# Reordering accumulating loads, sums of x and sums of weights in a pooled-attention and expert-mixture kernel

## The chip, the cores and the metric

The kernel runs on one core of a Trainium2 chip. The metric is the device time of one execution in microseconds (us), and lower is better. Quoted times are medians unless something else is said. PE is TensorE, PEld its weight loads, DVE is VectorE, ACT is ScalarE, POOL is GpSimd, SP is SyncE.

## The reference, cut to what matters

```python
def _attn_ref(q, k, v):                    # 8 batches x 8 heads, 576 rows, 64 columns
    k_p = k.reshape(B, H, Sp, 8, D).mean(axis=3)      # 72 pooled keys
    v_p = v.reshape(B, H, Sp, 8, D).mean(axis=3)      # 72 pooled values
    attn = softmax(q @ k_p.T / sqrt(D))
    return attn @ v_p

def _moe_ref(x, domain_probs, w1, w2):     # x 4608 x 512, 4 experts, 1024 hidden
    p = domain_probs / domain_probs.sum(-1)
    for e in range(4):
        out += p[:, e:e + 1] * (np.maximum(x @ w1[e], 0) @ w2[e])
```

The output of the attention is x of the mixture of experts.

## The kernel before

The two products of an expert are each done in seven smaller products instead of eight, which needs sums and differences of the operands beforehand. They are made by DVE: `weight_sums` and `first_weight_sums` of the weights, `x_sum` of x, `hidden_sums` of the hidden layer. All go through `combine`, a two-input DVE operation whose operands lie in SBUF.

The long middle of the kernel is a loop over slots. A slot holds one of the seven products of the "up" layer, in two halves, and one of the "down" layer of the expert before. 28 slots are one chunk of x (four experts), and under them runs the attention of the next batch: its loads, key and value sums, scores and contexts are hung onto slots by number. The engines each work in the order in which the program issues, so the slot number of a piece decides what stands ahead of it.

```python
def combine(dst, a, op, b):
    nc.vector.tensor_tensor(out=dst, in0=a, in1=b, op=op)

def load_part(b, what, part):      # parts 1.. add onto part 0, so each waits for the last
    src, raw = ((k, raw_k), (v, raw_v))[what]
    nc.gpsimd.dma_start(out=raw[:], in_=rows_of(src, b, 2 * part, 2 * part + 2),
                        accum_op=ALU.add if part else ALU.bypass)

def fold_keys(b, hs):              # (cut) two-input DVE operations in SBUF
    for dup in range(2):
        nc.vector.tensor_add(out=kp_all[0:SP, hs, dup, :], in0=raw[:, hs, 0, :],
                             in1=raw[:, hs, 1, :])

def hidden_sums(c, e, part):
    a11, a12, a21, a22 = quarters(c, e)
    if part == 0:
        combine(S3[:], a11, ALU.subtract, a21)      # called S below, 128x1024
    ...                                             # cut: parts 1 to 3

def down(c, e, step, flip=0, pooled=()):
    ...                                             # cut: eight matmuls into ps
    if step == 0:
        nc.scalar.copy(out=chains[(1 + flip) % 2][:], in_=chains[flip][:])
    elif step in pooled and e > 0:                  # pooled is (4,)
        for j in range(BLOCKS):
            prob = p_all[:, c * NR + row * BLOCKS + j, e:e + 1]
            nc.scalar.activation(out=addend[:, j], in_=ps[:, j], func=ACT.Copy, scale=prob)
        dst = acc[:, row * BLOCKS:(row + 1) * BLOCKS, cols]
        nc.gpsimd.tensor_add(out=dst, in0=dst, in1=addend[:])   # "the add of the step"
    else:
        ...                                         # cut: the same by DVE, from PSUM

# the slot loop, cut
for g in range(7 * N + 1):
    t, i = divmod(g, 7)
    if i in (0, 2, 3) and t < N:
        hidden_sums(*below_of[t], i)
    ...                                             # cut: two halves of an up product
    down(*below_of[t2], i2, t2 % 2, POOLED)
    for piece in later.get(g, ()):                  # attention of the next batch
        piece()
    for piece in sums.get(g, ()):                   # sums of weights
        piece()
```

Of each 28 slots, slots 5, 19 and 26 hold a `down` whose sum GpSimd adds. The add in slot 5 belongs to the last expert of the chunk before. GpSimd also issues the loads: a load that waits for an earlier landing holds up everything behind it in GpSimd's order.

The softmax here doesn't subtract the row's maximum and nothing guards it: scores larger than these inputs give would overflow.

## Time and profile before

| | before |
|---|---|
| time, median of 3 runs (range) | 500.82 us (499.92 to 501.33) |
| profiled span, granted clock | 498.8 us, 0.999 |
| PE busy, weight loads busy | 98%, 82% |
| DVE, ACT, POOL busy | 77%, 61%, 23% |

First the page of the profile. The busy line gives each engine's microseconds, its share and its instruction count. The chain of waits tells which engine's work ended last at each step. The last line is the group of GpSimd's adds of the step: 24 of them, 32.6 us in all, 1360 ns each.

```profile
PE 489.9 (98%) x4663; PEld 406.8 (82%) x4663; DVE 382.3 (77%) x756; ACT 303.3 (61%) x561; POOL 115.2 (23%) x112
...
PE 88%; DVE 9%; ACT 1%; issue 1%; ACTq 0%; DVEq 0%
...
L738 POOL TENSOR_TENSOR acc<-acc,addend 128x512 f32<-128x512 f32 x24 | 32.6, 1360 | 257.3 <-ACT addend L736 182.8
```

PE is the engine that bounds the kernel, but DVE holds 9% of the chain, which means places where PE waited for something that DVE delayed. The Trainium skill, page "Perfetto Trace Analysis", section "Identifying the Most-Contended Engine", advises MFU and the weight loads' busy share rather than matmul busy time. Here what is sought is below 1% of the time and lies in a few places. A share of the whole span doesn't say where they are: weight loads are busy 81.6% of the span. MFU was not worked out. The measure used here is the pace. In the steady stage a group of eight 128x256 matmuls starts 0.87 us after the group before, and any longer distance is a pause. Read so, PE paused 0.80 us at 245-247, 1.38 us at 298-300, 0.85 us at 437-441, 0.30 at 113, 0.32 at 85 and 0.49 at 67 and 75 together.

Each line is one stretch: its length, then busy time and instructions of PE, PEld, DVE, ACT and POOL, then clock and DMA.

```profile
core 0: us, PE busy (x) PEld busy (x) DVE busy (x) ACT busy (x) POOL busy (x), PEclk, DMA share, GB/s
...
95.00:130.00 35.00, 34.87 (x343) 29.93 (x343) 32.11 (x68) 22.34 (x40) 12.93 (x11) 1.00 0.73 71
...
230.00:285.00 55.00, 54.52 (x521) 47.23 (x520) 44.36 (x86) 35.05 (x66) 16.02 (x14) 1.00 0.65 81
285.00:340.00 55.00, 53.95 (x540) 46.34 (x538) 43.40 (x84) 35.46 (x66) 13.90 (x11) 1.00 0.55 73
340.00:440.00 100.00, 99.46 (x958) 87.60 (x956) 75.08 (x147) 61.49 (x118) 7.71 (x6) 1.00 0.13 30
```

Between 285 and 340 us PE lacks 1.05 us of a full stretch, between 230 and 285 it lacks 0.48. (Busy time hides a part, because the records overlap: that of a group lasts 1.03 us, and the next group starts 0.87 us after it. The pace is counted from start to start and does not.)

The timeline tells why. Columns are start, length, engine, line, operation, output and inputs, count, and in brackets the idle time before it with what ended that.

```profile
238.84 1.43 POOL L151 DMA_DIRECT2D kraw<-in_k_dram  x1 [1.31 <-DMA kraw<-in_k_dram]
...
239.69 0.84 ACT L736 ACTIVATE addend<-o_ps,p_all 128x256 f32<-128x256 f32 x2 [0.77 <-PE o_ps L724]
...
241.85 1.42 POOL L151 DMA_DIRECT2D vraw<-in_v_dram  x1 [1.58 <-DMA vraw<-in_v_dram]
...
242.60 2.52 DVE L242 TENSOR_TENSOR S<-H 128x1024 bf16<-128x1024 bf16 x1
242.71 1.84 POOL L738 TENSOR_TENSOR acc<-acc,addend 128x512 f32<-128x512 f32 x1
...
245.04 0.68 DVE L637 CUSTOM_DVE_ANT_0 H<-unit,partial 128x512 bf16<-128x512 f32 x1
...
245.80 0.57 ACT L669 COPY unit<-unit 128x512 f32<-128x512 f32 x1 [0.73 <-DVE H L637]
...
246.43 0.60 PE L656 MATMUL unit<-xT,w_bf 128*128 128x256 bf16 x4 [0.30 <-ACT unit L669]
...
247.21 1.03 PE L724 MATMUL o_ps<-w_bf,H 128*128 128x256 bf16 x8 [0.19 <-ACT o_ps L732]
```

ACT had the addend ready at 240.53 (239.69 + 0.84). GpSimd could not add it, for its queue held the third part of the values ahead of it, and that waited until 241.85 for the part before to land. So the add ran at 242.71. In that moment DVE began S, which then took 2.52 us. Everything behind S on DVE came late: the relu sum (L637), then ACT's copy of a PSUM bank (L669), and PE waited 0.30 us for that copy and 0.19 us for another. The same stood at 295, and S was worse there, although its record begins 0.69 us before that of the add:

```profile
294.91 1.40 POOL L151 DMA_DIRECT2D vraw<-in_v_dram  x1 [0.77 <-DVE acc L799]
...
295.08 3.08 DVE L242 TENSOR_TENSOR S<-H 128x1024 bf16<-128x1024 bf16 x1
...
295.77 1.83 POOL L738 TENSOR_TENSOR acc<-acc,addend 128x512 f32<-128x512 f32 x1
```

At 435 us it was a sum of x (128x512) that met the add; the same operation took 0.42 us when alone:

```profile
435.55 1.37 POOL L738 TENSOR_TENSOR acc<-acc,addend 128x512 f32<-128x512 f32 x1 [11.51 <-DVE H L637]
435.71 1.49 DVE L242 TENSOR_TENSOR xs<-x_rem,xs 128x512 bf16<-128x512 bf16 x1
```

At 109 us batch 3's key sums ran ahead of the add and were not held (0.75 us for two):

```profile
109.40 0.75 DVE L285 TENSOR_TENSOR kp<-kraw 72x512 bf16<-72x512 bf16 x2
...
110.07 0.68 DVE L242 TENSOR_TENSOR w_bf<-w_bf 128x1024 bf16<-128x1024 bf16 x1
110.16 1.72 POOL L738 TENSOR_TENSOR acc<-acc,addend 128x512 f32<-128x512 f32 x1 [5.01 <-DVE kp L285]
```

### The profile page before, as it was taken

To read this page: it belongs to the slowest core of one execution; us is meant where nothing else is said; L and a number is where in the kernel's file an instruction comes from. 1 tells how busy PE (TensorE), PEld (TensorE's weight loads), DVE (VectorE), ACT (ScalarE), POOL (GpSimd) and SP (SyncE) were. 2 spreads that over 40 slices of the span, in tenths; PEclk is the share of its full clock that TensorE was granted. 3 is DMA by queue.
4 is the path that set the end of the run, shared out by engine and by line. 5 is a ranking of instruction groups with operands and counts; after the bars stand their busy time and mean duration, and the time that the engine had idled before them with its cause. 6 is when DMAs were issued, how large, how long until landed. Compare 5 with 4: busy or idle time off the path is not lost.

```text
span 498.8 us, 11453 instructions
## 1 busy us (share of the span) xinstructions
PE 489.9 (98%) x4663; PEld 406.8 (82%) x4663; DVE 382.3 (77%) x756; ACT 303.3 (61%) x561; POOL 115.2 (23%) x112
## 2 busy tenths in 40 slices
PE   8999999999999999999999999999999999999996
PEld 5856458888888888888789878888888888888885
DVE  5567799899768976798769887896678766886674
ACT  4666536865775568556765666566665566556650
POOL 8320413233432164015501262111000100001010
PEclk9999999999999999999999999999999999999999
DMA  9999996987794569154945396220311010004003
GB/s 201 208 204 204 203 164 86 122 69 96 89 129 39 89 68 156 28 78 47 168 48 77 37 117 100 43 57 22 75 23 23 21 64 1 13 22 85 1 1 84
DMA packets 101779, 41.95 MB, mean 84 GB/s; under 512 B 73808, under 2 KB 100176, under 8 KB 101728
## 3 DMA queue, kind: packets, MB, share of 16 engines
q0 software_dynamic: 56896, 22.42, 39.8%
q1 hardware_dynamic: 43728, 17.77, 16.9%
q10 hardware_dynamic: 1104, 1.05, 0.6%
q8 instruction: 36, 0.59, 0.5%
q14 instruction: 15, 0.12, 0.1%
HBM read 45.69 MB, written 9.44 MB: 111 GB/s over the span
## 4 chain that ended last, share of the span: by engine, by line
PE 88%; DVE 9%; ACT 1%; issue 1%; ACTq 0%; DVEq 0%
PE o_ps L724 37%; PE unit L656 36%; PE unit L583 5%; DVE acc L799 3%; PE att L382 1%; PE o_ps L750 1%; DVE S L242 1%; PE unit L332 1%; PE att L435 1%; PE unit L782 1%; DVE H L637 1%; DVE wt_bf L242 1%; DVE x_tok L398 1%; DVE xs L242 1%; PE unit L598 0%
## 5 line engine op out<-in xcount | busy, mean ns | idle before, releaser
L799 DVE SCALAR_TENSOR_TENSOR acc<-o_ps,p_all,acc 128x256 f32<-128x256 f32 (+1 forms) x285 | 127.0, 486 | 55.3 <-PE o_ps L724 36.1
L724 PEld LDWEIGHTS <-H 128*128 128x128 bf16 x1320 | 129.0, 98 | 17.1 <-issue 1.2
L656 PEld LDWEIGHTS <-w_bf 128*128 128x128 bf16 x1024 | 97.7, 98 | 17.6 <-issue 6.1
L637 DVE CUSTOM_DVE_ANT_0 H<-unit,partial 128x512 bf16<-128x512 f32 x128 | 87.7, 685 | 24.7 <-PE unit L656 20.2
L724 PE MATMUL o_ps<-w_bf,H 128*128 128x256 bf16 x792 | 102.6, 272 | 0.5 <-ACT o_ps L732 0.4
L656 PE MATMUL unit<-xT,w_bf 128*128 128x256 bf16 x672 | 96.4, 273 | 1.3 <-ACT unit L669 1.3
L738 POOL TENSOR_TENSOR acc<-acc,addend 128x512 f32<-128x512 f32 x24 | 32.6, 1360 | 257.3 <-ACT addend L736 182.8
L671 ACT COPY partial<-unit 128x512 f32<-128x512 f32 x128 | 72.0, 590 | 32.8 <-PE unit L656 32.6
L656 PEld LDWEIGHTS <-wu_bf 128*128 128x128 bf16 x768 | 73.3, 98 | 10.0 <-issue 1.5
L656 PE MATMUL unit<-xs,wu_bf 128*128 128x256 bf16 x512 | 76.9, 273 | 0.0
L724 PE MATMUL o_ps<-wt_bf,H 128*128 128x256 bf16 x528 | 68.4, 273 | 0.0
L724 PEld LDWEIGHTS <-S 128*128 128x128 bf16 x528 | 51.7, 98 | 6.4
L677 ACT ACTIVATE H<-unit 128x512 bf16<-128x512 f32 x64 | 38.2, 597 | 29.3 <-PE unit L656 29.0
L673 ACT ACTIVATE H<-unit 128x512 bf16<-128x512 f32 x64 | 38.8, 606 | 27.4 <-PE unit L656 27.4
L669 ACT COPY unit<-unit 128x512 f32<-128x512 f32 x64 | 37.3, 582 | 19.3 <-PE unit L656 14.9
L656 PE MATMUL unit<-xs,w_bf 128*128 128x256 bf16 x256 | 38.5, 273 | 0.0
L797 ACT ACTIVATE acc<-o_ps,p_all 128x256 f32<-128x256 f32 x72 | 30.3, 472 | 12.0 <-PE o_ps L724 10.4
L151 POOL DMA_DIRECT2D kraw<-in_k_dram x20 | 25.4, 1270 | 42.1 <-DMA kraw<-in_k_dram 42.1
L724 PE MATMUL o_ps<-w_bf,S 128*128 128x256 bf16 x264 | 34.2, 273 | 0.0
L724 PE MATMUL o_ps<-wt_bf,S 128*128 128x256 bf16 x264 | 34.2, 273 | 0.0
L656 PE MATMUL unit<-xT,wu_bf 128*128 128x256 bf16 x224 | 33.6, 272 | 0.0
L151 POOL DMA_DIRECT2D vraw<-in_v_dram x20 | 26.9, 1343 | 22.6 <-DMA vraw<-in_v_dram 21.8
(148 smaller groups left out, 522.3 us busy)
## 6 DMA issues: line engine op xcount, KB each, us to landing
out_dram<-acc SPq DMA_DIRECT2D x32, 256.0 KB, 4.2
w_bf<-in_moe_w_dram POOLq DMA_DIRECT2D x7, 1024.0 KB, 24.1
q_sb<-in_q_dram POOLq DMA_DIRECT2D x7, 512.0 KB, 9.7
vraw<-in_v_dram POOLq DMA_DIRECT2D x22, 144.0 KB, 5.8
kraw<-in_k_dram POOLq DMA_DIRECT2D x21, 144.0 KB, 5.3
w_bf<-in_moe_w_dram POOLq DMA_DIRECT2D x2, 512.0 KB, 8.5
wt_bf<-in_k_dram POOLq DMA_DIRECT2D x2, 288.0 KB, 6.7
wt_bf<-in_v_dram POOLq DMA_DIRECT2D x4, 144.0 KB, 5.1
```

The lines of the kernel that those rows point to most:

```text
L151: nc.gpsimd.dma_start(out=raw[:], in_=rows_of(src, b, 2 * part, 2 * part + 2), accum_op=ALU.add if part else ALU.bypass)
L583: nc.tensor.matmul(out_ps, lhsT=w1_bf[:, e, kc, fc * P:(fc + 1) * P], rhs=xT[:, kc, at], start=(kc == 0), stop=(kc == KC - 1), skip_group_ ...
L637: nc.vector._custom_dve(TENSOR_ADD_SAT, out=dst, in0=ps, in1=part, s0=LARGEST, s1=0.0)
L656: nc.tensor.matmul(ps[:, n * HN:(n + 1) * HN], lhsT=lhs[:, kc, f:f + P], rhs=rhs[:, kc, :], start=(not grows and n == 0 and kc == 0), stop ...
L669: nc.scalar.copy(out=units[unit][1][:], in_=ps)
L671: nc.scalar.copy(out=part[:, step - 2], in_=ps)
L673: nc.scalar.activation(out=quarter(0, 0), in_=ps, func=ACT.Relu)
L677: nc.scalar.activation(out=quarter(0, 1), in_=ps, func=ACT.Relu)
L724: nc.tensor.matmul(ps[:, j], lhsT=lhs[:, i, j * P:(j + 1) * P], rhs=rhs[:, i, :], start=(not grows and i == 0 and j == 0), stop=(i == HF - 1),
L738: nc.gpsimd.tensor_add(out=dst, in0=dst, in1=addend[:])
L797: nc.scalar.activation(out=dst, in_=o_ps, func=ACT.Copy, scale=prob)
L799: nc.vector.scalar_tensor_tensor(out=dst, in0=o_ps, scalar=prob, in1=dst, op0=ALU.mult, op1=ALU.add,)
```

## The change

The intent is to let GpSimd's add of the step run before the later load parts of the same slot, so that it is over when DVE's S begins; to bring the sums of x ahead of the add in the last slots; and to spread sums of weights, which stood in bunches around batch 1's contexts, singly over DVE's idle places. No work is added or removed: both kernels have 11453 instructions.

```diff
--- before.py
+++ after.py
@@ -850,6 +850,8 @@
                 if 4 <= i < 7:
                     sums[1][i - 4]()
                     sums[2][i - 4]()
+                if i == 5:
+                    sums[1][3]()
                 if i == 6:
                     fold_keys(1, every)
         down(0, 0, 6)
@@ -878,8 +880,10 @@
         load_q_rem(0)
         load_q_rem(1)
         load_wide(1, 2)
+        each(*weight_sums(1)[0:1])
         down_plain(0, 1, 0)
         scores(1, 3)
+        each(*weight_sums(1)[1:2])
         down_plain(0, 1, 1)
         context(1, 0)
         down_plain(0, 1, 2)
@@ -888,14 +892,13 @@
         down_plain(0, 1, 3)
         context(1, 2)
         turn(1, 1)
-        each(*weight_sums(1)[0:2])
         down_plain(0, 2, 0)
         context(1, 3)
         turn(1, 2)
-        each(*weight_sums(1)[2:3], sums[1][3])
+        each(*weight_sums(1)[2:3])
         down_plain(0, 2, 1)
         turn(1, 3)
-        each(*weight_sums(3)[0:2])
+        each(*weight_sums(3)[0:3])
         down_plain(0, 2, 2)
         each(*(lambda n=n: x_sum(1, n) for n in range(4)))
 
@@ -909,15 +912,15 @@
 
         usual = dict(
             queries=-8, keys=-9, values=-2, scores=(-1, 3, 5, 6), contexts=(11, 14, 18, 21),
-            q=1, k=(-2, 0, 3, 6), v=(-2, 0, 3, 6), x=(22, 25, 25, 26), rem=(-3, 17, 24, 25),
+            q=1, k=(-2, 0, 5, 9), v=(-2, 0, 5, 9), x=(22, 25, 25, 25), rem=(-3, 17, 24, 25),
         )
         plans = {b: usual for b in range(BUSY, B + 1)}
         plans[BUSY] = dict(
-            queries=0, keys=4, values=12, scores=(11, 12, 13, 15), contexts=(16, 18, 20, 21),
-            q=6, k=(5, 8, 11, 14), v=(13, 16, 19, 24), x=(24, 26, 26, 26), rem=(0, 6, 8, 14),
-        )
-        plans[B] = dict(usual, x=(25, 25, 26, 26), rem=(-3, 17, 21, 22))
-        plans[BUSY + 1] = dict(usual, values=4, v=(5, 8, 11, 14))
+            queries=0, keys=4, values=12, scores=(11, 12, 13, 15), contexts=(16, 18, 19, 21),
+            q=6, k=(5, 8, 11, 14), v=(13, 16, 19, 24), x=(24, 25, 25, 25), rem=(0, 6, 8, 14),
+        )
+        plans[B] = dict(usual, x=(24, 24, 25, 25), rem=(-3, 17, 21, 22))
+        plans[BUSY + 1] = dict(usual, values=4, v=(5, 8, 12, 16))
 
         for b, plan in plans.items():
             start = 7 * E * (b - BUSY)
@@ -991,7 +994,7 @@
         later = pieces_later()
         below_of = [(0, 3)] + order
         sums = {}
-        for at, pieces in (((5, 3), weight_sums(3)[2:]), ((7,), first_weight_sums(2)[3:]), ((8,), weight_sums(1)[3:]), ((12, 15, 22, 19), weight_sums(2)),
+        for at, pieces in (((3,), weight_sums(3)[3:]), ((7,), first_weight_sums(2)[3:]), ((8,), weight_sums(1)[3:]), ((12, 15, 22, 19), weight_sums(2)),
                            ((15,), first_weight_sums(3)[3:])):
             for slot, piece in zip(at, pieces, strict=True):
                 sums.setdefault(slot, []).append(piece)
```

## The prediction

> **What bounds it now.** TensorE (PE): 98% of the 498.8 us span, granted clock 0.999; the chain of waits is 88% PE. In the steady stage eight 128x256 matmuls start every 0.87 us, so only PE's pauses can be won, and each passes whole to the end (VectorE, DVE, is 77% busy). From the timeline I took, per group of matmuls, the next start minus this start minus the normal pace. The pauses are: 0.80 us at 245-247, 1.38 at 298-300, 0.85 at 437-441, 0.3 at 113, 0.3 at 85, 0.5 together at 67 and 75. Sum 4.1 us. (The fill until 34 us is left alone.)
>
> **Why they pause.** The two large ones are a collision. GpSimd's add of the step (acc+addend, 1.27 us alone) stood in its queue behind the third parts of keys and values, each of which waits for the landing of the part before. The addend was ready at 240.5, but the add ran 242.71-244.55, just when DVE began the S difference (both inputs in SBUF): 2.52 us instead of 0.68; at 295.1, 3.08. At 190 the same op took 1.75 us with no pause behind it. What stands behind S frees a PSUM bank late (PE waits for ScalarE's unit copy, 0.3 and 0.86 us). At 435.7 the last x sum took 1.49 instead of 0.42 for the same reason. The Trainium skill ("SBUF — State Buffer", section "Who interferes with whom") says that a DVE instruction with two SBUF inputs contends with a GpSimd instruction that reads SBUF and that the loser blocks wholly. The trace agrees: all five long ops overlap an add; 28 DVE differences of this size that overlap only a load's issue took 0.69 us at most.
>
> **What the change does.** No work added or removed.
> - Loads go behind the add: it should run at about 240.6-241.9 and 293.1-294.4, ahead of S at 242.6 and 295.1. Wins 0.80+1.38. Parts 3 and 4 start a few us later, still over 10 us before their fold.
> - x one slot sooner: the sums of the last chunk end before the add at 435.4. Its transpose has landed by about 429.7, the sums want it at 432. Wins 0.85.
> - Weight sums spread: about 1.3 us of DVE work moves into its idle gaps at 42, 56 and 58 us. Wins most of the 0.5 at 67/75 and, with one sum out of the stretch at 83, the 0.3 at 85. Context one slot sooner: wins 0.2-0.3 at 113.
> - Loss expected, 0.5 us: near 110 us the earlier context pushes batch 3's key copies (two SBUF inputs) into the add at 110.0, blocking DVE up to 1 us where it is 98% busy.
>
> Net 3.6 us of 500.8 (0.7%): **497.2 us, 80% range 496.0 to 499.2**; faster by over 2%: 0.01, within 2%: 0.98, slower by over 2%: 0.01.
>
> **What would show it.** The slot's adds near 189, 241, 293 us last about 1.3 us; every S difference 0.7 us; no PE wait on ScalarE's unit copy near 245, 298, 437; the x sums at 433 each 0.42 us; PE's pauses after 60 us below 1 us in all.
>
> **What would make it wrong.** The add collides with another two-input DVE op (the slot's x sums, key copies), moving the pause rather than curing it; a moved weight sum delays a PSUM release (68-75 us) or an x sum waits for its transpose; or pauses I read as additive were absorbed later.

## The result

| | before | after |
|---|---|---|
| time, median (range), 6 runs each | 501.1 (499.92 to 501.33) | 497.53 us (497.28 to 498.73) |
| profiled span, granted clock | 498.8, 0.999 | 495.8 us, 0.998 |
| ratio of fast runs, 95% interval | | 0.9938 (0.9923 to 0.9952) |

The six of the kernel before include the three quoted above, which is why its median differs from theirs. A ratio is the mean time of one kernel's fast runs over that of the other's in the same rounds, so it is not quite the ratio of the medians: the ratio says 3.1 us of 501, the medians differ by 3.57 us. The prediction's 497.2 us is 0.3 us below the median measured, and its range holds it.

The page after: PE's share of the chain rose to 95%, DVE's fell to 2%, and the mean add is 95 ns shorter.

```profile
PE 488.6 (99%) x4663; PEld 407.1 (82%) x4663; DVE 377.1 (76%) x756; ACT 302.7 (61%) x561; POOL 114.4 (23%) x112
...
PE 95%; DVE 2%; ACT 1%; issue 1%; ACTq 0%
...
L738 POOL TENSOR_TENSOR acc<-acc,addend 128x512 f32<-128x512 f32 x24 | 30.4, 1265 | 258.3 <-ACT addend L736 201.3
```

Windows after, in the same columns. The two stretches from 230 to 340 us and the one from 340 to 440 us are now full. The one from 95 to 130 us lost 0.66 us of PE's busy time (34.87 before).

```profile
95.00:130.00 35.00, 34.21 (x336) 29.49 (x334) 32.44 (x66) 21.91 (x39) 12.37 (x11) 1.00 0.75 71
...
230.00:285.00 55.00, 55.00 (x529) 47.99 (x527) 42.69 (x86) 35.72 (x68) 16.05 (x15) 1.00 0.69 83
285.00:340.00 55.00, 55.00 (x552) 47.40 (x552) 42.56 (x86) 35.96 (x67) 13.77 (x11) 1.00 0.53 72
340.00:440.00 100.00, 100.00 (x964) 88.46 (x965) 74.97 (x149) 62.27 (x119) 7.61 (x6) 1.00 0.11 30
```

The slot at 241 us. The add follows its addend at once and takes 1.26 us; both loads come behind it; S takes 0.68 us; PE has no wait at 245-247.

```profile
240.70 1.26 POOL L738 TENSOR_TENSOR acc<-acc,addend 128x512 f32<-128x512 f32 x1 [3.17 <-ACT addend L736]
...
241.91 1.42 POOL L151 DMA_DIRECT2D kraw<-in_k_dram  x1
...
242.64 0.68 DVE L242 TENSOR_TENSOR S<-H 128x1024 bf16<-128x1024 bf16 x1
242.81 1.97 POOL L151 DMA_DIRECT2D vraw<-in_v_dram  x1
...
243.24 0.69 DVE L637 CUSTOM_DVE_ANT_0 H<-unit,partial 128x512 bf16<-128x512 f32 x1
...
245.01 0.59 ACT L669 COPY unit<-unit 128x512 f32<-128x512 f32 x1
...
246.44 1.04 PE L724 MATMUL o_ps<-w_bf,H 128*128 128x256 bf16 x8
```

Note the load issue that began 0.17 us after S and lay over it and the relu sum behind it: neither got longer. At 433 us the last sum of x ends before the add begins:

```profile
432.33 0.42 DVE L242 TENSOR_TENSOR xs<-x_rem,xs 128x512 bf16<-128x512 bf16 x1
...
433.42 1.27 POOL L738 TENSOR_TENSOR acc<-acc,addend 128x512 f32<-128x512 f32 x1 [11.51 <-DVE H L637]
```

At 109-113 us stands something new. The add now begins 0.14 us ahead of batch 3's key sums, these take 1.74 us, and the relu sum behind them releases ACT's copy late; PE waits 0.79 us for it.

```profile
109.42 1.26 POOL L738 TENSOR_TENSOR acc<-acc,addend 128x512 f32<-128x512 f32 x1 [4.13 <-ACT addend L736]
109.56 1.74 DVE L285 TENSOR_TENSOR kp<-kraw 72x512 bf16<-72x512 bf16 x2
...
111.83 0.67 DVE L637 CUSTOM_DVE_ANT_0 H<-unit,partial 128x512 bf16<-128x512 f32 x1
...
112.59 0.57 ACT L669 COPY unit<-unit 128x512 f32<-128x512 f32 x1 [2.41 <-DVE H L637]
113.21 1.03 PE L656 MATMUL unit<-xT,w_bf 128*128 128x256 bf16 x8 [0.79 <-ACT unit L669]
```

To put a number on each place, I compared the start of the same group of matmuls in both profiles, and took how much that shift changes between marks chosen in stretches without pauses. Because the shift stays constant between the places named, each pause passed whole to the end. The fill (until 34 us) is left out: its shift is anything from -0.26 to +0.82 us among the profiles, by chance.

| profile against before's, us | 34-92: weight sums | 92-124: keys at 110 | 124-228: S at 190 | 228-281: S at 243 | 281-335: S at 295 | 418-487: x sum at 435 | sum |
|---|---|---|---|---|---|---|---|
| after | -0.68 | +0.80 | -0.03 | -0.80 | -1.37 | -0.84 | -2.92 |

### The profile page after: what moved, and what is told of

The parts are those of the page before. It is cut to its first block, busy times and chain, and to the rows that moved or that the text cites. A ratio compares the mean times of both kernels' runs of the same rounds, so it can differ in the third digit from the quotient of the medians.

```text
span 495.8 us, 11453 instructions
## 1 busy us (share of the span) xinstructions
PE 488.6 (99%) x4663; PEld 407.1 (82%) x4663; DVE 377.1 (76%) x756; ACT 302.7 (61%) x561; POOL 114.4 (23%) x112
## 3 DMA queue, kind: packets, MB, share of 16 engines
q10 hardware_dynamic: 1104, 1.05, 0.6%
## 4 chain that ended last, share of the span: by engine, by line
PE 95%; DVE 2%; ACT 1%; issue 1%; ACTq 0%
PE o_ps L724 40%; PE unit L656 39%; PE unit L583 5%; PE o_ps L750 3%; PE att L382 2%; PE unit L332 1%; PE unit L782 1%; PE att L435 1%; DVE acc L799 1%; PE unit L598 0%; PE unit L306 0%; DVE H L637 0%; DVE kp L285 0%; PE att L489 0%; PE att L472 0%
## 5 line engine op out<-in xcount | busy, mean ns | idle before, releaser
L738 POOL TENSOR_TENSOR acc<-acc,addend 128x512 f32<-128x512 f32 x24 | 30.4, 1265 | 258.3 <-ACT addend L736 201.3
L151 POOL DMA_DIRECT2D vraw<-in_v_dram x20 | 29.3, 1466 | 24.1 <-DMA vraw<-in_v_dram 23.8
```

## The experiments

The theory: GpSimd's add and a two-input DVE operation hold each other up; for S this costs PE time when the add stands directly behind a load in GpSimd's queue; four parts of the change (loads, sums of x, weight sums, context) act separately. The rivals: that the load traffic or its issue slows DVE, with the add a bystander; that the gain of the loads comes from the other moves; that a busy GpSimd is enough, whatever it does. Each kernel was correct, and each is compared with runs of the kernel before on the same chip. The table above continued, from one profile each (sums can be 0.01 off by rounding):

| profile against before's, us | 34-92 | 92-124 | 124-228 | 228-281 | 281-335 | 418-487 | sum |
|---|---|---|---|---|---|---|---|
| loads alone | 0 | 0 | -0.03 | -0.80 | -1.37 | 0 | -2.21 |
| all but the loads | -0.68 | +0.80 | +0.91 | 0 | -0.43 | -0.85 | -0.25 |
| weight sums alone | -0.68 | 0 | +0.01 | -0.15 | -1.36 | 0 | -2.19 |
| context alone | 0 | +0.80 | +0.34 | -0.28 | 0 | 0 | +0.86 |
| last x sums alone | 0 | disturbed | +0.52 | -0.12 | -1.36 | -0.85 | - |
| before, three adds by DVE | 0 | 0 | +0.25 | -0.80 | -1.37 | -0.85 | -2.77 |
| after, add delayed | -0.68 | +0.80 | -0.03 | -0.81 | -1.36 | -0.85 | -2.93 |
| after, keys and a weight sum later | -0.68 | +0.12 | -0.03 | -0.80 | -1.37 | -0.84 | -3.61 |
| after, keys later | -0.70 | +0.80 | -0.03 | -0.80 | -1.36 | -0.85 | -2.94 |
| after, three pieces moved | -0.84 | -0.28 | -0.03 | -0.81 | -1.36 | -0.85 | -4.17 |

### The loads alone, on the kernel before

```diff
-            q=1, k=(-2, 0, 3, 6), v=(-2, 0, 3, 6), x=(22, 25, 25, 26), rem=(-3, 17, 24, 25),
+            q=1, k=(-2, 0, 5, 9), v=(-2, 0, 5, 9), x=(22, 25, 25, 26), rem=(-3, 17, 24, 25),
-        plans[BUSY + 1] = dict(usual, values=4, v=(5, 8, 11, 14))
+        plans[BUSY + 1] = dict(usual, values=4, v=(5, 8, 12, 16))
```

> The kernel before with only the parts of keys and values moved behind the add (slots 5 and 9 in place of 3 and 6). Theory (collision of GpSimd's add with VectorE's S difference): the pauses of PE near 246 and 299 us vanish, the adds of those steps last 1.27 us and every S difference 0.7 us; the pauses at 67, 75, 85, 113 and 437 stay. Shift against before: 0 until 240, -0.8 after 250, -2.2 after 302 and at the end, about 498.9 us where before is 501.1. Rival (the gain is spread over the whole change, the loads only change when DMA traffic comes): under 1 us, or shifts that begin elsewhere than at 245 and 298.

Measured: 498.3 us (498.02 to 499.03), ratio 0.9963 (0.9947 to 0.9979), which is 1.9 us. S took 0.68 us at 242.69, and the two pauses at 245 and 298 are gone. The loads alone are the larger part of the gain, and no other place changed.

### All but the loads

```diff
-            q=1, k=(-2, 0, 5, 9), v=(-2, 0, 5, 9), x=(22, 25, 25, 25), rem=(-3, 17, 24, 25),
+            q=1, k=(-2, 0, 3, 6), v=(-2, 0, 3, 6), x=(22, 25, 25, 25), rem=(-3, 17, 24, 25),
-        plans[BUSY + 1] = dict(usual, values=4, v=(5, 8, 12, 16))
+        plans[BUSY + 1] = dict(usual, values=4, v=(5, 8, 11, 14))
```

> The changed kernel with the loads put back to slots 3 and 6. Theory: the two collisions come back, S differences of about 2.5 and 3.1 us (and 1.75 near 190 without a pause), so 2.2 us slower than the changed kernel, about 499.7; it keeps -0.7 until 109, loses it at 113, and wins 0.85 at 437. Rival (the moved sums have given VectorE enough slack to swallow a late S): no pause at 246 and 299 although S is long, time as the changed kernel within 0.5 us.

Measured: 500.53 us (499.62 to 500.97), ratio 1.0002 (0.9987 to 1.0018). The other moves alone gain nothing measurable: -0.68 and -0.85 are eaten by the +0.80 at 113 us and the +0.91 at 190 us. For with the old order of the loads, S was held at 190 too (1.97 us beyond its 0.68), at 243 the same as before (1.85) and at 295 less (1.96). Its slot at 244 us:

```profile
244.28 2.53 DVE L242 TENSOR_TENSOR S<-H 128x1024 bf16<-128x1024 bf16 x1
244.40 1.84 POOL L738 TENSOR_TENSOR acc<-acc,addend 128x512 f32<-128x512 f32 x1
```

So with the old load order, how far S is held varies from one execution to the next; what goes with it is shown in the section on why the prediction was right or wrong.

### The add delayed, in the kernel after

```diff
             dst = acc[:, row * BLOCKS:(row + 1) * BLOCKS, cols]
+            if e == E - 1 and c in (3, 4):
+                for _ in range(2):
+                    nc.gpsimd.tensor_copy(out=addend[:], in_=addend[:])
             nc.gpsimd.tensor_add(out=dst, in0=dst, in1=addend[:])
```

> The changed kernel, loads left behind the add, but in the fourth expert's step of chunks 3 and 4 GpSimd first copies the addend onto itself twice (same result), so that the add starts about 2 us later, near S again. Theory (it is the add's moment that counts, not the order of the loads): S differences there of about 2 us or more, PE pauses of 0.5 to 1.4 us each, 1.2 to 2.6 us slower than the changed kernel. Rival (what counts is where the loads stand in the queue and when they run): S stays at 0.7 us, no pause, time as the changed kernel.

Measured: 497.3 us (497.27 to 498.09), ratio 0.9945 (0.9930 to 0.9959); no pause. This is a miss as an experiment. The delay brought the add only 0.55 us ahead of S, so S was held for 0.58 us, and that much is absorbed:

```profile
242.56 1.27 POOL L741 TENSOR_TENSOR acc<-acc,addend 128x512 f32<-128x512 f32 x1
...
243.11 1.26 DVE L242 TENSOR_TENSOR S<-H 128x1024 bf16<-128x1024 bf16 x1
```

It gives points of the rule below, but it tells the theories apart no further. An add with no load ahead of it could hardly have done more: it lasts 1.27 us, and S ends 0.55 us after it, so an S of 0.68 us can lose at most about 1.1 us to it (an estimate from these three numbers). The rule below puts what is absorbed at 1.03 us.

### The add held longer, in the kernel after (run twice)

```diff
             dst = acc[:, row * BLOCKS:(row + 1) * BLOCKS, cols]
+            if e == E - 1 and c in (3, 4):
+                nc.gpsimd.tensor_copy(out=addend[:], in_=addend[:])
+                nc.gpsimd.tensor_add(out=addend[:], in0=addend[:], in1=addend[:])
+                nc.gpsimd.tensor_scalar_mul(out=addend[:], in0=addend[:], scalar1=0.5)
             nc.gpsimd.tensor_add(out=dst, in0=dst, in1=addend[:])
```

> After the miss of the late add (S only 0.58 us long over its normal time, no pause): so far six collisions with S fit one rule, pause of PE = S's excess minus 1.03 us (excess 1.84 gave 0.80, 2.40 gave 1.38, 1.07 at 190 and 0.58 in the last run gave none). Now GpSimd has four ops in a row there, copy, doubling, halving (exact), add, so that it is at work from 241.2 to about 245.0 while S comes at 243.1; loads stand behind as in the changed kernel. Theory: S waits to the end of the last, excess about 1.9 us, pause about 0.85 us at each of the two places, 1.7 us slower than the changed kernel, with the loads in the changed order. Rival (order and time of the loads): S at most 0.6 us long over normal and no pause. Open: whether S can slip in between two GpSimd ops; then the excess is about 0.6 us or less and nothing is told apart.

Measured: five runs at 497.53 to 498.47 us and one, the profiled one, at 1023.01 us: TensorE went at about half pace in it (0.50 us a matmul of 256 columns in place of 0.27), with a granted clock of 1.0; why stays open. Its profile can't be compared. The ratio of the fast runs is 0.9951 (0.9934 to 0.9969). The same kernel was therefore run once more:

> The kernel with four GpSimd ops in a row again, since its first profile fell into an execution at half TensorE speed. Its five fast runs (497.5 to 498.5 us) are not 1.7 us slower than the changed kernel, so I now expect that S slips in between two of GpSimd's ops: S at most 0.6 us over its normal time, no pause of PE near 245 and 298, and the add itself held until S has read. If S is nevertheless 1.9 us over, the rule excess minus 1.03 us must show 0.85 us of pause at each place, or the rule falls.

Measured: 497.56 us in the profiled run, four runs with median 498.86 us, ratio 0.9982 (0.9945 to 1.0019); no pause at 246 or 299. GpSimd was busy from 240.50 to 245.19 with gaps of 0.1 us, and yet S, which began inside the third of its four operations, lost only 0.37 us:

```profile
242.33 1.51 POOL L741 TENSOR_SCALAR addend<-addend 128x512 f32<-128x512 f32 x1
242.43 1.05 DVE L242 TENSOR_TENSOR S<-H 128x1024 bf16<-128x1024 bf16 x1
...
243.92 1.27 POOL L742 TENSOR_TENSOR acc<-acc,addend 128x512 f32<-128x512 f32 x1
```

So a busy GpSimd is not enough, not even with four operations in a row that read SBUF; this rival falls, in the form tried. The operation that lay over S was the halving, which reads one operand. It was not slowed either: it took 1.49 and 1.51 us in the profile of the first run too, where no DVE operation with two operands in SBUF met it. A longer add with two operands across S was not tried. And two of the four runs took 499.97 and 500.97 us; they have no profile, so the absence of pauses is shown for the fastest run only. My attempt to bring the collision back by delaying the add alone failed in both forms.

### The add taken from GpSimd, on the kernel before

This leaves the loads in their old slots and gives three adds (the last expert's, of chunks 2 to 4) to DVE, which does them in 0.88 us in an idle place of 0.95 us. ACT's two operations that made the addend go as well.

```diff
-        elif step in pooled and e > 0:
+        elif step in pooled and e > 0 and not (e == E - 1 and c in (2, 3, 4)):
```

> The kernel before, loads in their old slots 3 and 6, but the fourth expert's step of chunks 2, 3 and 4 is added by VectorE from PSUM (0.88 us) instead of ScalarE and GpSimd: no add of GpSimd near S, order of the loads untouched. Theory (collision): every S difference 0.7 us, no pause at 246 and 299, 2.2 us faster than before, as with the loads moved; VectorE idled 0.95 us just there. Rival (the place of the loads is what costs): the pauses of 0.80 and 1.38 us stay, time as before.

Measured: 497.94 us (497.78 to 500.17), ratio 0.9965 (0.9946 to 0.9984). The pauses at 246 and 299 are gone, by the same 0.80 and 1.37 us as with the loads moved. The third part of the values is issued under S as before, and S keeps its 0.68 us:

```profile
238.49 1.43 POOL L151 DMA_DIRECT2D kraw<-in_k_dram  x1 [1.03 <-DMA kraw<-in_k_dram]
...
242.17 1.42 POOL L151 DMA_DIRECT2D vraw<-in_v_dram  x1 [2.25 <-DMA vraw<-in_v_dram]
...
242.59 0.68 DVE L242 TENSOR_TENSOR S<-H 128x1024 bf16<-128x1024 bf16 x1
```

This decides between the add and the loads. The issue or the traffic of the load isn't what holds S; the add is, in the place into which the load pushes it. Two side effects had not been foreseen: the pause at 437 us was also gone (the DVE work ahead of the last x sums ran earlier, and the last of these sums began at 433.18, 0.19 us ahead of an add, and took 0.42 us: here the one that began first was not held), and a new one of 0.28 us appeared at 206 us.

### The sums of x of the last chunk alone, on the kernel before

```diff
-        plans[B] = dict(usual, x=(25, 25, 26, 26), rem=(-3, 17, 21, 22))
+        plans[B] = dict(usual, x=(24, 24, 25, 25), rem=(-3, 17, 21, 22))
```

> The kernel before with only the x sums of the last chunk one slot sooner. Theory: the x sum that took 1.49 us takes 0.42, PE's pauses of 0.85 us at 437 and 441 vanish, all else stays, 0.85 us faster than before at the end (500.2 where before is 501.1). Rival (the gain needs the other parts): no shift or a pause elsewhere after 430.

Measured: 500.26 us (499.4 to 505.44), ratio 1.0021 (0.9984 to 1.0058). Two of six runs were disturbed (505.44 and 503.68 us), the profiled one among them: its clock fell in one slice near 120 us. The times therefore settle nothing. In its profile the place at 437 us gained 0.85 us, which is the whole of what the change gained there. At 295 us S was not held in this execution, at 190 and 243 it was, by 1.58 and 1.72 us.

### The weight sums alone

The edit is the change without the loads, the sums of x and the context. Against the kernel after:

```diff
-            q=1, k=(-2, 0, 5, 9), v=(-2, 0, 5, 9), x=(22, 25, 25, 25), rem=(-3, 17, 24, 25),
+            q=1, k=(-2, 0, 3, 6), v=(-2, 0, 3, 6), x=(22, 25, 25, 26), rem=(-3, 17, 24, 25),
...                  # and the three plans below it, all as in the kernel before
```

> The kernel before with only the weight sums moved. From the ledger of the changed kernel: 0.26 us won at 67, 0.11 at 75, 0.31 at 85, so 0.7 us earlier from 87 us on and at the end; pauses at 113, 246, 299 and 437 as before. Rival (the pauses at 67 to 85 go with another part of the change): under 0.3 us there.

Measured: 499.65 us (498.68 to 502.02), ratio 0.9995 (0.9975 to 1.0015). The profile shows -0.68 us between 34 and 92 us; the times, with an interval of 2 us, can't confirm it.

### The context one slot sooner alone, on the kernel before

```diff
-            queries=0, keys=4, values=12, scores=(11, 12, 13, 15), contexts=(16, 18, 20, 21),
+            queries=0, keys=4, values=12, scores=(11, 12, 13, 15), contexts=(16, 18, 19, 21),
```

> The kernel before with only the context of batch 2 in slot 19 in place of 20. Theory: it puts the key copies under GpSimd's add at 110 (copies 1.7 us in place of 0.75 us), pause of about 1 us at 113 in place of 0.3, so 0.7 to 0.8 us slower than before from 114 us on. Rival (it only needs the other moves to pay): no long key copies, 0.2 to 0.3 us won at 113.

Measured: 501.37 us (500.69 to 501.91), ratio 1.0024 (1.0011 to 1.0038): slower by about 1.2 us. The key sums took 1.74 us under an add that began 0.13 us ahead of them, as in the kernel after, and the place cost 0.80 us. So the new pause of the kernel after comes from this one line, and from no other part.

### Keys and one weight sum a slot later, in the kernel after

```diff
-        plans[BUSY + 1] = dict(usual, values=4, v=(5, 8, 12, 16))
+        plans[BUSY + 1] = dict(usual, keys=-8, values=4, v=(5, 8, 12, 16))
-        for at, pieces in (..., ((12, 15, 22, 19), weight_sums(2)),
+        for at, pieces in (..., ((12, 15, 22, 20), weight_sums(2)),
```

> The changed kernel with batch 3's key copies and the last weight sum of expert 2 one slot later (slot 20), so that VectorE has the relu sum and the accumulation, with one SBUF tensor each, under GpSimd's add at 109.4 to 110.7. Theory (the new pause of 0.99 us at 113 comes from key copies blocked by the add): key copies 0.75 us for both in place of 1.74, no PE pause at 113, all later times 0.9 to 1.0 us earlier, about 496.6 us. Rival (the earlier context overloads VectorE there, whatever the add does): the work only moves, the pause stays above 0.5 us or turns up at S some 2 to 4 us later.

Measured: 496.8 us (496.57 to 498.57), ratio 0.9937 (0.9920 to 0.9954). The key sums run after the add and take 0.74 us; a relu sum, which has only one operand in SBUF, lies under the add and keeps its 0.68 us. The place costs 0.12 us instead of 0.80, because DVE is now behind by 0.34 us at 114.3.

### Keys alone a slot later, in the kernel after

```diff
-        plans[BUSY + 1] = dict(usual, values=4, v=(5, 8, 12, 16))
+        plans[BUSY + 1] = dict(usual, keys=-8, values=4, v=(5, 8, 12, 16))
```

> The changed kernel with only the key copies of batch 3 one slot later; the weight sum (two SBUF inputs) stays and so comes first under the add at 109.4. Theory (collision): the weight sum takes about 1.75 us in place of 0.68, the relu sum behind it starts at about 111.3 in place of 111.8, so PE's pause at 113 falls only from 0.99 to about 0.4 us; 0.5 us faster than the changed kernel. Rival (too much VectorE work ahead of the relu sum, no blocking): the weight sum takes 0.68 us, the pause is gone.

Measured: 497.44 us (497.27 to 497.86), ratio 0.9941 (0.9924 to 0.9958). This is a miss in size: the key sums were free, but the weight sum moved up into their place and was held instead, so the pauses only moved to 115 us: the place costs +0.80 us, as in the kernel after.

```profile
109.51 1.26 POOL L738 TENSOR_TENSOR acc<-acc,addend 128x512 f32<-128x512 f32 x1 [4.51 <-ACT addend L736]
109.64 1.68 DVE L242 TENSOR_TENSOR w_bf<-w_bf 128x1024 bf16<-128x1024 bf16 x1
```

### Three pieces moved, in the kernel after

```diff
-        each(*weight_sums(3)[0:3])
+        each(*weight_sums(3)[0:2])
-        plans[BUSY + 1] = dict(usual, values=4, v=(5, 8, 12, 16))
+        plans[BUSY + 1] = dict(usual, keys=-8, values=4, v=(5, 8, 12, 16))
-        for at, pieces in (((3,), weight_sums(3)[3:]), ..., ((12, 15, 22, 19), weight_sums(2)),
+        for at, pieces in (((2, 3), weight_sums(3)[2:]), ..., ((12, 15, 22, 15), weight_sums(2)),
```

> The changed kernel with the key copies of batch 3 in slot 20, the last weight sum of expert 2 in slot 15, where VectorE idles 0.77 us, and the third weight sum of expert 3 in slot 2 in place of ahead of the first x sums. Expect: no pause of PE over 0.15 us after 70 us; against the last variant (keys and sum in slot 20) another 0.34 us at 114 and 0.15 us at 74; 1.3 us faster than the changed kernel, about 496.2 us. If VectorE is short of time there, a pause at 85 or 105 us comes back and it is no faster than that variant.

Measured: 496.76 us (496.52 to 497.11), ratio 0.9927 (0.9912 to 0.9943). No pause is left after 70 us. By the table it is 1.25 us better than the kernel after (-4.17 against -2.92). It was run at another time. The timings agree in direction, but their intervals overlap, so a gain over the kernel after is shown by the profiles and not by the times. It is the best version found, and it beats the kernel before clearly.

## Why the prediction was right or wrong

The size of the whole was right: 3.6 us predicted, 3.1 by the ratio, 2.9 between 34 us and the end by the profiles. Point by point:

- **The collision at 243 and 295.** Predicted 0.80 and 1.38 us, measured 0.80 and 1.37. That it takes the add behind the load is shown from both sides: the loads moved alone, and the add given to DVE with the loads left in place, take away the same two pauses.
- **How a held S becomes a pause.** Over the thirteen held S of the five profiles with the old order of loads and adds, the pause is the excess of S over 0.68 us, less 1.02 to 1.05 us: 1.84 gave 0.80, 2.40 gave 1.38, 1.97 gave 0.93, 1.41 gave 0.37. Smaller excesses gave hardly any (1.07 at 190 us before: 0.03) or none (0.58 with the delayed add). This is why the held S at 190 us cost next to nothing before.
- **What sets the excess of S.** These five profiles hold fifteen places where an add stands directly behind a load near S. In the thirteen in which S was held it began 0.17 to 1.51 us after the start of the load's issue, and it ended 1.85 or 1.86 us after the end of that issue each time. In the other two S began 0.14 us after the start of the issue (last x sums alone, at 302) or 0.01 us before it (weight sums alone, shown here) and took its usual time:

```profile
294.69 0.68 DVE L242 TENSOR_TENSOR S<-H 128x1024 bf16<-128x1024 bf16 x1
...
294.70 1.40 POOL L151 DMA_DIRECT2D vraw<-in_v_dram  x1 [0.90 <-DMA vraw<-in_v_dram]
```

By these fifteen, what counts is whether S begins before or after a moment some 0.15 us behind the start of the load's issue, and not the start of the add's record: so the S at 295 was held although it began before that record. The prediction went by the moment of the add alone.
- **The sums of x.** Predicted 0.85 us, measured 0.84, and 0.85 by that part alone.
- **The weight sums.** Predicted most of 0.5 us at 67/75 and 0.3 at 85, measured 0.37 and 0.31, 0.68 together; 0.16 us near 75 stayed.
- **The context one slot sooner: the step that failed.** The prediction put "Loss expected, 0.5 us" against a gain of "0.2-0.3 at 113", net a loss of about 0.25 us. The mechanism was right, batch 3's key sums ran into the add at 110 us. The term was mis-sized: the place cost 0.80 us net, in the change and alone. The gain at 113 us did not come, since DVE, held 1 us, released ACT's copy later than before. With it failed one of the signs that the prediction had named, PE's pauses after 60 us below 1 us in all: 0.16 us at 74 and 1.07 us at 113 and 116 were left.
- **"Each pause passes whole to the end."** Held: the shift is constant between the places in every profile.

One doubt on the size of the main term. The kernel before doesn't lose the same in each execution. In the five profiles with the old order of loads and adds (before, all but the loads, and x sums, weight sums and context alone, one of them disturbed), the pauses of the three slots add up to 2.2, 2.7, 1.2 (the disturbed one), 0.7 and 2.3 us, mean 1.8 us; these kernels differ in other parts too, so the spread is a hint. The profile on which the prediction rested shows 2.2. The timed ratio of the loads alone is 1.9 us, with an interval from 1.1 to 2.7. So the sum from one profile, 3.6 us less the mis-sized 0.55 us, may still overstate the mean gain a little; that the total came so close to the prediction is in part the luck of this draw. The scatter of the times doesn't decide it: the six runs of the kernel before range over 1.41 us, those of the kernel after over 1.45 us.

What stays open: why S is held from the first 0.15 us of the load's issue on, when an issue with no add behind it holds nothing (S 0.68 us with the adds taken from GpSimd). The add's record begins 0.86 or 0.87 us after the issue's in all fifteen places, so an earlier start of the add that no record shows would fit as well. That an add behind a load lasts 1.83 us is no sign of a hold: it does so too where S was not held (302.97 and 295.56 us in the two cases above), and its record begins 0.53 to 0.55 us before the issue's ends and ends 1.29 or 1.30 us after it. A held 128x1024 operation ended 0.55 to 0.56 us after the add's record had, whenever it began; a smaller one (a sum of x, the second key sum) 0.28 us. Also open is what moves the load's issue from one execution to the next: in five of the fifteen places the trace names the landing of the part before as what it waited for, in the others an ACT or DVE operation.

## What to carry to other kernels

An engine far from being the bottleneck can still cost time by the moment at which it runs: look at the operations that take far longer than their group's usual time and ask which other engine's operation lies across them. When a piece is moved, look at what moves up into its place and at what then runs beside the other engine's operation; here one moved line cost 0.80 us because two-input sums slid under an add. Where an operation waits its turn behind a load's issue, compare start times with that of the issue too. And where a loss depends on a collision, one profile is one draw: take several before giving it a size.

## What the Trainium skill lacked or had wrong

- Page "SBUF — State Buffer", section "Who interferes with whom": it says that a DVE instruction with two SBUF inputs contends with a GpSimd instruction that reads SBUF. The runs agree: S 2.52 us instead of 0.68 (128x1024), key sums 1.74 instead of 0.75, a sum of x 1.49 instead of 0.42. A relu sum with one operand in SBUF kept 0.68 us under an add.
- The same section says that whoever issues first blocks the other for a whole instruction. By the records of the two operations that doesn't fit everywhere: S began at 295.08, the add at 295.77, and S ended at 298.16, 0.56 us after the add. In all fifteen places with an add directly behind a load it fits if the start of the load's issue is taken for the add's turn: S beginning 0.17 us or more after it was held, S beginning 0.14 us after it or sooner was not. The page has no word on this.
- The same section infers that a DVE sum of two SBUF inputs takes only the read interface of the shared pair, while the issue of a load needs the write interface. The runs agree in that such a sum was not held by an issue alone: 0.68 us with a load's issue lying over it, and at most 0.69 us in the 30 such cases of the kernel before (the prediction counted 28).
- By the same section the loser blocks wholly. S under the halving did not: it began 0.10 us after it, lost 0.37 us and ended 0.35 us before it did. The section has no case of GpSimd operations in a row.
- Page "Perfetto Trace Analysis", section "Identifying the Most-Contended Engine": the weight loads' busy share, 81.6% before and 82.1% after, doesn't tell in which places a gain of 0.6% lies. The distance from start to start of equal groups of matmuls did: 0.87 us without a pause, and each pause could be read off as what was over that.
